# A planned order for chunk attention and a leaky-ReLU layer on one core: another load order at the start, half-wide first products, and copies planned apart from sums

## The chip, the core and the metric

The kernel runs on one core of a Trainium2 chip. The metric is the device time of one execution in microseconds (us); lower is better. The core has TensorE (PE in the profile) for matmuls, VectorE (DVE), ScalarE (ACT), GpSimd (POOL) and SyncE (SP), which each run their own list of instructions in order, and 16 DMA engines that are fed from queues. The loads are issued by POOL, the transposing copies and the stores by SP.

## The reference

```python
# q, k, v: (8, 8, 576, 64) float32; w_in: (512, 2048); w_out: (2048, 512)
def attn(q, k, v):                      # in chunks of 64 rows
    scores = (1 / sqrt(64)) * q_c @ k_c.T
    scores = scores - max(scores, axis=-1)
    attn = exp(scores); attn = attn / (sum(attn, axis=-1) + 1e-9)
    return attn @ v_c
x = attn_out.transpose(0, 2, 1, 3).reshape(4608, 512)
h = x @ w_in
g = maximum(0.01 * h, h)
out = (g @ w_out).astype(float32)
```

There are 72 chunks for each of 8 heads, and 4608 tokens go through the two layers. Inside the kernel the operands are float16, the sums float32.

## The kernel before

**Tiling.** A *group* u (0 to 35) is 128 tokens, two chunks of 64, all 8 heads. It goes through a chain of steps, each one instruction or a few: the loads (`arrive`, lines 776 to 782); the transposes of q and k, `pe_t`, on TensorE for u below `UD` = 10 (lines 400 to 408) and by a DMA on SP for the others (`t`, lines 421 to 432); the copies of the transposed q into a zero-padded tile QZ (`p`, lines 410 and 441); the scores `s` on TensorE (line 445, tile Sp); the largest value `m` and the difference `b` on VectorE; the exponential `x` on ScalarE; the sum and its reciprocal `z` on VectorE; the product `n` on VectorE or POOL (line 482, tile en); the transpose of the weights, `e` on TensorE and `d2` as its copy out, or `d` by a DMA on SP (lines 490 to 508, tile et); the product with v, `v` (line 510, tile xp); and `a` on ScalarE, which writes the 128 tokens into the ring xT (line 526).

**The two layers.** Tokens are handled in `BLOCKS`: four of 128 and eight of 512. Blocks 0 to 5 multiply plainly with w_in (`mm1`, line 176, 16 matmuls that are 128 columns wide), blocks 6 to 11 with a seven-product scheme (`f`, lines 307 to 325) that works on sums of quarter matrices: VF and WF are sums of the weights, XF sums of tokens (`x_form`, line 277), S sums of the hidden layer (`g_form`, line 336). Before the change a seven-product unit covers all 512 tokens of a block, so that one product is 4 matmuls of 256 columns. The second layer is plain for blocks 0 to 3 (`mm2`, line 205, in four parts of 4 matmuls, one for each quarter of w_out) and has the seven-product scheme for the others (`m2`, line 351, 8 matmuls of 256 columns).

**What sets the order.** Every step is an object with an engine, an assumed duration, the steps that it comes after, and a key. `run()` (line 626) plays the whole program with these durations and a model of the DMA queues, takes for each engine the ready step with the smallest key, and emits the instructions in that order. The result is a fixed list for each engine. On the chip each engine then follows its list, and waits wherever the data are not there. `TUNE` shifts keys and adds delays to single steps, `ON` moves single steps to another engine (it is empty before). Where the plan sees TensorE idle for over 0.4 us in its first 40 us, it puts in *fillers*: matmuls of the identity on itself (`idle`, line 531) whose results nothing uses.

**The start.** `front()` (line 795) gives the order of the first loads. A letter stands for a load: `Q` a quarter of w_in (two transfers of 256 KB in the tile), `P` a quarter of w_out (512 KB), `V` a 128-token tile of v that is then copied into place in eight or four pieces (`v_p`, line 128), `g` q and k of a group (128 KB each), `v` the v of the whole second batch, and `I` the identity, which all the transposes and fillers need. Group 0's q and k come by two other queues as float32.

Of the kernel before, what the change touches and what calls it, by code (L numbers as in the profile page):

```python
# [16 lines left out]
def kernel(  # L17
# [23 lines left out]
    UD = 10  # L41
# [11 lines left out]
    UNIT = {}  # L53
    POOL_N, POOL_X, POOL_S = 9, 20, 20
# [45 lines left out]
    def load_q(u):  # L100
        load_rows(q_tile(u), q, u)
        qk[u] = (q_tile(u), None)
# [127 lines left out]
    def minus(to, a, b):  # L230
        nc.vector.tensor_tensor(out=to, in0=a, in1=b, op=ALU.subtract)

    def plus(to, a, b):
        nc.vector.tensor_tensor(out=to, in0=a, in1=b, op=ALU.add)  # L234
# [5 lines left out]
    def out_form(i):  # L240
        if i == 0:
            minus(WF[:, 0], B12, B11)
        elif i == 1:
            minus(WF[:, 1], B22, WF[:, 0])
        elif i == 2:
            minus(WF[:, 2], B22, B12)
        else:
            minus(WF[:, 3], B21, WF[:, 1])
# [6 lines left out]
    def in_form(i):  # L255
        if i == 0:
            plus(VF[:, 0], W21, W22)
        elif i == 1:
            minus(VF[:, 1], VF[:, 0], W11)
        elif i == 2:  # L260
            minus(VF[:, 2], W11, W21)
        else:
            minus(VF[:, 3], W12, VF[:, 1])
# [362 lines left out]
    def run():  # L626
# [14 lines left out]
        of = {"pool": 0, "sp": 1}  # L641

# [43 lines left out]
        while True:  # L686
# [32 lines left out]
            now[s.eng] = s.issued  # L719
            can[s.eng].remove(s)  # L720
# [21 lines left out]
    FILL, FILL_TO, NEAR = 0.8, 40.0, 0.12  # L742
# [6 lines left out]
    TUNE = {('out', 0, 0): (-1, 0), ('pe_t', 8, 1): (2, 0), ('v', 5): (2, 0), ('s', 4): (-2, 0), ('m', 1): (0, 0.8), ('g', 1, 2, 0): (8, 1.2), ('mm2', 2, 0, 1): (0, 0.15), ('z', 5): (-4, 0), ('mm1', 2, 3, 0): (8, 0), ('pe_t', 5, 1): (2, 0), ('zv', 2, 0): (8, 0), ('a', 0): (-2, 0.5), ('b', 3): (0, 0.3), ('mm1', 0, 3, 0): (-8, 0), ('z', 2): (-8, 0), ('mm2', 3, 0, 0): (-2, 0), ('g', 2, 2, 0): (8, 0), ('v_p', 4, 1): (-1, 0), ('pe_t', 5, 0): (0, 0.8), ('v_p', 6, 1): (4, 0), ('v_p', 2, 0): (0, 1.2), ('mm2', 1, 0, 1): (0, 0.15)}  # L749
# [39 lines left out]
    ON = {}  # L789
# [5 lines left out]
    def front():  # L795
        for what in "Q0 I V0 g1 Q1 q2 k2 g3 V1 V2 Q2 P0 g4 V3 Q3 P1 P2 g6 g5 V4 v1 g7 P3".split():
# [3 lines left out]
            elif what[0] in "gqk":  # L800
                for i in ((0, 1) if what[0] == "g" else (0,) if what[0] == "q" else (1,)):
                    arrive(n[0], i)
            elif what[0] == "v":
                arrive_v(n[0], *(n[1:] or (0, NCH)))
            elif what[0] == "V":
                n = n[0]
                cs = [c for c in (2 * n, 2 * n + 1) if c < NCH]
                load(("v_t", n), 0.88, lambda n=n: load_v_rows(n), 510 * len(cs))
# [10 lines left out]
        for n, more in ((1, 500), (4, 700)):  # L819
# [9 lines left out]
        for i in range(4):  # L829
            for t in range(4):  # L830
                e, us = on(("zv", i, t), "dve", dve=0.3, act=0.6, pool=0.35)
                add(("zv", i, t), e, us, lambda i=i, t=t, e=e: zero(empty(i)[:, t], e, i % 2 * CH), key=8, at=(2.0, 2.5, 14.0, 14.0)[i])

    def group(u):
        at = 44.0 + BEGIN + (u - 5) * PACE if u >= 5 else 0.0
        k = u / 4
        dve = act = 10 + k - 1 * max(0, 5 - u)
# [23 lines left out]
        else:  # L861
            if not pairs:
                add(("t", u, 0), "sp", 1.28, lambda u=u: stage_t(u, 2), [get(("arrive", u, 0)), get(("p", u - 4, 0)), get(("p", u - 4, 1))], key=u).dmas = [(544, 1.0)]
                for s in range(2):
                    add(("p", u, s), "pool", 0.68, lambda u=u, s=s: stage_q2(u, s), [get(("t", u, 0)), get(("s", u - NQZ))], key=u / 100).slack = 0.0
# [21 lines left out]
        if by_pe:  # L887
# [12 lines left out]
        add(("v", u), "pe", 0.24, lambda u=u, h=h: stage_v(u, h.slot), need, key=-2, take=[h]).slack = 0.0 if by_pe else 1.0  # L900
# [116 lines left out]
    def second_fast(j, k0):  # L1017
# [4 lines left out]
        f2 = add(("sf", j, 2), *(("pool", 4.0) if j >= POOL_S else ("dve", 1.25)), lambda: g_form(j, 2), [f0] + g(0, 0), key=6.2 + k0)  # L1022
# [79 lines left out]
    BEGIN, PACE, SPARE, SPARE2, LEAN, LIMIT = -4, 4.8, 0, 0, 0.6, 3  # L1102
    front()
    for q_ in range(4):
        add(("wf", q_), "dve", 1.24, lambda q_=q_: out_form(q_), [get(("P", i)) for i in range(4)], key=9 + q_ / 10, at=44.0 + 8.0 + 3 * q_)
    for q_ in range(4):
        add(("vf", q_), "dve", 1.5, lambda q_=q_: in_form(q_), [get(("Q", 3, m)) for m in range(2)], key=9.5 + q_ / 10, at=44.0 + 8.0 + 15 + 3 * q_)
# [86 lines left out]
```

## Time and profile before

| | us |
|---|---|
| median of 3 runs | 280.42 (280.1 to 280.96) |
| the profiled execution | 279.68 |
| its span, first to last instruction | 277.5 |
| TensorE busy in the span | 266.2 (96%) |
| VectorE busy | 216.4 (78%) |
| ScalarE busy | 189.9 (68%) |
| POOL busy | 161.8 (58%) |

The page gives, for each engine, the time in which at least one of its instructions ran. Loads of weights into TensorE (PEld) run beside its matmuls (PE). A busy TensorE here includes the 135 fillers. In the rows of the timeline the columns are: start, duration, engine, line, operation, output and inputs, count of merged instructions, and in brackets the idle time before it and what ended that. A matmul's duration in a row is longer than its turn in the pipe, so the turn is read from one start to the next.

### The profile page before, as it was taken

What the parts mean: (1) busy time and instruction counts of PE and PEld (TensorE: products, weight loads), DVE (VectorE), ACT (ScalarE), POOL (GpSimd) and SP (SyncE); (2) the same over time, 40 slices, a digit from 0 to 9 for tenths busy, and PEclk for the clock granted to TensorE, in tenths of its full rate; (3) what the DMA queues carried; (4) which work ended last, traced back from release to release, by engine and by line L of the source; (5) the groups of instructions that cost most, each with busy time, mean ns of one, the idle gap of its engine ahead of it and who ended that gap; (6) DMA issues with size and microseconds to landing.
All of it is one profiled execution on the core that took longest, in us unless ns stands there. A gap on an engine that the chain in (4) does not pass through costs nothing.

```text
span 277.5 us, 7926 instructions
## 1 busy us (share of the span) xinstructions
PE 266.2 (96%) x3231; PEld 237.8 (86%) x3231; DVE 216.4 (78%) x382; ACT 189.9 (68%) x359; POOL 161.8 (58%) x194
## 2 busy tenths in 40 slices
PE   4899999999989999999999999999999999999995
PEld 3799957897988899989889988998999998888884
DVE  8678746999799959979997899799879963753372
ACT  3358854874763563799699749976977985795521
POOL 8765858729999999895976687775172210000000
PEclk9999999999999999999999999999999999999999
DMA  8999999999999999999999999999995210400133
GB/s 132 164 171 185 189 157 173 157 176 135 185 140 155 123 144 158 139 233 139 189 191 139 136 224 155 155 179 139 152 184 117 93 21 2 151 2 1 76 116 115
DMA packets 164180, 38.79 MB, mean 140 GB/s; under 512 B 155184, under 2 KB 159792, under 8 KB 164144
## 3 DMA queue, kind: packets, MB, share of 16 engines
q0 software_dynamic: 114384, 18.09, 102.7%
q1 hardware_dynamic: 48720, 19.93, 42.6%
q8 instruction: 25, 0.41, 0.6%
q10 hardware_dynamic: 1040, 0.26, 0.4%
q14 instruction: 11, 0.09, 0.1%
HBM read 36.70 MB, written 9.44 MB: 166 GB/s over the span
## 4 chain that ended last, share of the span: by engine, by line
PE 81%; DMA 6%; DVE 6%; POOL 3%; issue 1%; ACT 0%; DVEq 0%; POOLq 0%
PE oA L370 18%; PE hA L322 14%; PE hT L184 14%; PE oC L370 9%; PE hC L322 7%; PE oP L209 5%; PE hB L322 3%; PE oB L370 3%; DMA et<-en 3%; DMA k_in<-in_k_dram 3%; PE Sp L450 3%; PE xp L516 3%; DVE S L234 2%; DVE XF L282 1%; POOL w_inT L134 1%
## 5 line engine op out<-in xcount | busy, mean ns | idle before, releaser
L370 PEld LDWEIGHTS <-gT 128*128 128x128 f16 x640 | 61.5, 98 | 6.9
L184 PE MATMUL hT<-xT,w_inT 128*128 128x128 f16 x768 | 47.5, 219 | 0.3
L486 POOL TENSOR_TENSOR en<-ex,zi 128x512 f16<-128x512 f16 x27 | 29.7, 1102 | 29.6 <-DVE zi L480 16.3
L443 POOL COPY QZ<-QT 64x512 f16<-64x512 f16 x52 | 38.3, 737 | 12.5 <-DMA QT<-q_in 10.8
L184 PEld LDWEIGHTS <-w_inT 128*128 128x128 f16 x768 | 43.9, 98 | 1.4 <-PE idle L534 0.5
L322 PEld LDWEIGHTS <-VF 128*128 128x128 f16 x384 | 36.8, 98 | 4.7 <-issue 0.4
L234 DVE TENSOR_TENSOR tmp<-hC,tmp 128x512 f32<-128x512 f32 x48 | 31.9, 680 | 10.7 <-ACT tmp L198 5.3
L92 POOL DMA_DIRECT2D k_in<-in_k_dram x39 | 33.4, 859 | 6.9 <-DMA k_in<-in_k_dram 3.3
L92 POOL DMA_DIRECT2D q_in<-in_q_dram x39 | 33.5, 859 | 6.2 <-DMA q_in<-in_q_dram 1.4
L195 ACT ACTIVATE gT<-hT 128x512 f16<-128x512 f32 x48 | 28.1, 596 | 11.4 <-PE hT L184 10.9
L195 ACT ACTIVATE gT<-tmp 128x512 f16<-128x512 f32 x48 | 29.4, 640 | 7.0 <-DVE tmp L234 6.8
L470 ACT ACTIVATE ex<-sh 128x512 f16<-128x512 f32 x36 | 22.7, 630 | 14.2 <-DVE sh L464 10.3
L370 PE MATMUL oA<-WF,gT 128*128 128x256 f16 x256 | 31.7, 273 | 0.0
L198 ACT ACTIVATE tmp<-hA 128x512 f32<-128x512 f32 x48 | 28.2, 607 | 4.0 <-PE hA L322 4.0
L460 DVE TENSOR_REDUCE mx<-Sp 128x8 f32<-128x512 f32 x36 | 24.4, 678 | 7.7 <-PE Sp L450 7.3
L476 DVE TENSOR_REDUCE z<-ex 128x8 f32<-128x512 f16 x36 | 24.4, 677 | 7.7 <-ACT ex L470 7.6
L322 PEld LDWEIGHTS <-w_inT 128*128 128x128 f16 x288 | 27.6, 98 | 3.1
L529 ACT ACTIVATE xT<-xp 128x512 f16<-128x512 f32 x36 | 21.6, 599 | 11.5 <-PE xp L516 11.5
L322 PE MATMUL hA<-XF,VF 128*128 128x256 f16 x192 | 28.0, 273 | 0.0
L370 PEld LDWEIGHTS <-S 128*128 128x128 f16 x256 | 24.4, 98 | 3.6 <-DVE S L234 0.9
L198 ACT ACTIVATE tmp<-oA 128x512 f32<-128x512 f32 (+1 forms) x27 | 14.8, 547 | 17.9 <-PE oA L370 17.8
L464 DVE TENSOR_TENSOR sh<-Sp,mx 128x512 f32<-128x512 f32 x36 | 24.4, 679 | 0.4
(69 smaller groups left out, 491.6 us busy)
## 6 DMA issues: line engine op xcount, KB each, us to landing
out_dram<-osb SPq DMA_DIRECT2D x14, 512.0 KB, 5.7
VB<-in_v_dram POOLq DMA_DIRECT2D x14, 288.0 KB, 10.7
q_in<-in_q_dram POOLq DMA_DIRECT2D x31, 128.0 KB, 10.1
k_in<-in_k_dram POOLq DMA_DIRECT2D x31, 128.0 KB, 10.1
w_inT<-in_moe_w_in_dram POOLq DMA_DIRECT2D x8, 256.0 KB, 7.6
w_outT<-in_moe_w_out_dram POOLq DMA_DIRECT2D x4, 512.0 KB, 9.5
out_dram<-osb SPq DMA_DIRECT2D x6, 256.0 KB, 5.7
v_t<-in_v_dram POOLq DMA_DIRECT2D x4, 128.0 KB, 8.2
```

The costliest lines, as they stand in the source:

```text
L92: nc.gpsimd.dma_start(out=t[a - u * G:z - u * G], in_=src[b, :, r:r + z - a, :].rearrange("h p d -> p h d"))
L184: nc.tensor.matmul(out=hT[:, i, :], lhsT=w_inT[:, t, fc * 128:(fc + 1) * 128], rhs=xT[:, t, r0 % RING:r0 % RING + tb], start=(i == 0 and t ...
L195: nc.scalar.activation(out=to, in_=of, func=AFT.Prelu, bias=0.0, scale=1.0, alpha=0.01)
L198: nc.scalar.activation(out=to, in_=of, func=AFT.Copy, bias=0.0, scale=1.0)
L234: nc.vector.tensor_tensor(out=to, in0=a, in1=b, op=ALU.add)
L322: nc.tensor.matmul(out=PA[key][:, c, :], lhsT=w[:, t, fc * 128:(fc + 1) * 128], rhs=x[:, t, :], start=(m in (1, 5) and c == 0 and t == 0), ...
L370: nc.tensor.matmul(out=to, lhsT=lhs[:, fc, p * 128:(p + 1) * 128], rhs=rhs[:, fc, :], start=(fresh and fc == 0), stop=(fc == HB - 1), skip ...
L443: nc.gpsimd.tensor_copy(out=QZ[u % NQZ][part, :, :, s, :], in_=QT[u][part].rearrange("p i (e t) -> p i e t", e=2))
L460: nc.vector.tensor_reduce(out=MX[u], in_=SP[u], axis=AXL.X, op=ALU.max)
L464: nc.vector.tensor_tensor(out=SH[u], in0=SP.pop(u), in1=MX.pop(u).unsqueeze(2).to_broadcast((128, 8, CH)), op=ALU.subtract)
L476: nc.vector.tensor_reduce(out=z, in_=E[u], axis=AXL.X, op=ALU.add)
L486: eng.tensor_tensor(out=E[u], in0=ex, in1=ZI.pop(u).unsqueeze(2).to_broadcast((128, 8, CH)), op=ALU.mult)
```

## The change

1. **Start.** The load order becomes q1 k1 k2 Q0 I q2 q3 V0 V1 V2 k3 Q1 Q2 q5 V3 q4 P0 and so on: three groups' q and k ahead of most weights, the identity behind the first five transfers, Q3 near the end. Each part of `mm2` waits only for its own quarter of the hidden layer. The copies of v into place, the zeroing of tiles and the copies of q are spread over ScalarE, VectorE and POOL by `ON`.
2. **Fillers.** Their number is worked out from two rates: one for TensorE's slow first 4.3 us after the identity is there, one for afterwards. There are 86 in place of 135.
3. **Ports.** In the plan, POOL's copies and products (`p`, `n`, `v_p`, `zv`, `zq`) and VectorE's float16 sums (`wf`, `vf`, `sf`, `xf`) never run at the same time: a step with the flag `port` begins when the other engine's last such step has ended. No wait is added in the program for it.
4. **Width.** `UNIT` = 256 for blocks 6 to 11: a seven-product unit covers 256 tokens. A product is 8 matmuls of 128 columns; the sums XF are 48 instructions of 256 elements in place of 24 of 512.
5. **Engines.** `UE` = 8: the transposes `e` of groups 8 and 9 go from TensorE to a DMA on SP. VectorE makes 12 of the products `n` in place of 9, POOL 24 in place of 27. The slack that the plan keeps between a DMA transpose and the step `v` goes from 1.0 to 0.5 us.
6. **Pace and keys.** `BEGIN, PACE` = -6, 5.0 in place of -4, 4.8; `NEAR` 0.03 in place of 0.12; `TUNE` has entries over the whole program in place of its start alone.

```diff
-    UD = 10
+    UD, UE = 10, 8
...
-    UNIT = {}
-    POOL_N, POOL_X, POOL_S = 9, 20, 20
+    UNIT = {6: 256, 7: 256, 8: 256, 9: 256, 10: 256, 11: 256}
+    POOL_N, POOL_X, POOL_S = 10, 20, 20
...
-            return t
+            return max(t, port["dve" if s.eng == "pool" else "pool"]) if s.port else t
...
+            warm = done["I"].end + 4.3 if done["I"].end else INF
+            if s.eng == "pe" and t < warm:
+                s.us *= 1.8
...
-                    idle(int((t - a) * FILL / (0.0575 if a > done["I"].end + 4.5 else 0.12)), k[1])
+                    idle(int(max(0, min(t, warm) - a - 0.1) / 0.1065 + max(0, t - max(a, warm)) * FILL / 0.0575), k[1])
...
+            if s.port:
+                port[s.eng] = s.issued
...
+        s.port = s.eng == "dve" and name[0] in ("wf", "vf", "sf", "xf") or s.eng == "pool" and name[0] in ("p", "n", "v_p", "zv", "zq", "sf", "xf")
...
-        for what in "Q0 I V0 g1 Q1 q2 k2 g3 V1 V2 Q2 P0 g4 V3 Q3 P1 P2 g6 g5 V4 v1 g7 P3".split():
+        for what in "q1 k1 k2 Q0 I q2 q3 V0 V1 V2 k3 Q1 Q2 q5 V3 q4 P0 k5 P1 k4 q6 k7 V4 P2 k6 q7 Q3 v1 P3".split():
...
-        if by_pe:
+        if u < UE:
             h = Hold("bank")
             add(("e", u), "pe", 0.23, lambda u=u, h=h: stage_e(u, h.slot), [get(("n", u))], key=-2, take=[h])
...
-        add(("v", u), "pe", 0.24, lambda u=u, h=h: stage_v(u, h.slot), need, key=-2, take=[h]).slack = 0.0 if by_pe else 1.0
+        add(("v", u), "pe", 0.24, lambda u=u, h=h: stage_v(u, h.slot), need, key=-2, take=[h]).slack = 0.0 if by_pe else 0.5
...
-                        [s, get(("P", part))] + [x for key, v in G_OF.items() if key[0] == j for x in v], key=at, take=[hd] if part == 0 else [], spare=SPARE)
+                        [s, get(("P", part)), get(("g", j, part, 0))], key=at, take=[hd] if part == 0 else [], spare=SPARE)
...
-    BEGIN, PACE, SPARE, SPARE2, LEAN, LIMIT = -4, 4.8, 0, 0, 0.6, 3
+    BEGIN, PACE, SPARE, SPARE2, LEAN, LIMIT = -6, 5.0, 0, 0, 0.6, 3
```

More of the change, by code (lines that the diff above doesn't have):

```diff
@@ L101, in load_q @@
         load_rows(q_tile(u), q, u)
[L102 removed]
+        qk[u] = (q_tile(u), qk[u][1] if u in qk else None)
     def load_k(u):
@@ L641, in run @@
         of = {"pool": 0, "sp": 1}
+        port = {"dve": 0.0, "pool": 0.0}
         def release(s, which):
@@ L748 @@
     Step.slack = Step.hold = 0.0
-    TUNE = {('out', 0, 0): (-1, 0), ('pe_t', 8, 1): (2, 0), ('v', 5): (2, 0), ('s', 4): (-2, 0), ('m', 1): (0, 0.8), ('g', 1, 2, 0): (8, 1.2), ('mm2', 2, 0, 1): (0, 0.15), ('z', 5): (-4, 0), ('mm1', 2, 3, 0): (8, 0), ('pe_t', 5, 1): (2, 0), ('zv', 2, 0): (8, 0), ('a', 0): (-2, 0.5), ('b', 3): (0, 0.3), ('mm1', 0, 3, 0): (-8, 0), ('z', 2): (-8, 0), ('mm2', 3, 0, 0): (-2, 0), ('g', 2, 2, 0): (8, 0), ('v_p', 4, 1): (-1, 0), ('pe_t', 5, 0): (0, 0.8), ('v_p', 6, 1): (4, 0), ('v_p', 2, 0): (0, 1.2), ('mm2', 1, 0, 1): (0, 0.15)}
+    Step.port = False
@@ L807, in front @@
                 cs = [c for c in (2 * n, 2 * n + 1) if c < NCH]
-                load(("v_t", n), 0.88, lambda n=n: load_v_rows(n), 510 * len(cs))
+                load(("v_t", n), 0.88, lambda n=n: load_v_rows(n), 560 * len(cs))
                 for c in cs:
@@ L818, in front @@
                 load(("P", n[0]), 1.0, lambda a=n[0]: load_w_out(a), 2930)
-        for n, more in ((1, 500), (4, 700)):
+        for n, more in ((1, 500), (4, 700)) if arrivals[0].name[0] != "Q" else ((0, 1300), (1, -200)):
             arrivals[n].dmas = [(p + more / len(arrivals[n].dmas), y) for p, y in arrivals[n].dmas]
@@ L831, in front @@
                 e, us = on(("zv", i, t), "dve", dve=0.3, act=0.6, pool=0.35)
-                add(("zv", i, t), e, us, lambda i=i, t=t, e=e: zero(empty(i)[:, t], e, i % 2 * CH), key=8, at=(2.0, 2.5, 14.0, 14.0)[i])
+                add(("zv", i, t), e, us, lambda i=i, t=t, e=e: zero(empty(i)[:, t], e, i % 2 * CH), key=8, at=(2.0, 2.5, 20.0, 22.0)[i])
     def group(u):
@@ L836, in group @@
         k = u / 4
-        dve = act = 10 + k - 1 * max(0, 5 - u)
+        dve = act = 10 + k - 0.5 * max(0, 5 - u)
         by_pe = u < UD
@@ L864, in group @@
                 for s in range(2):
-                    add(("p", u, s), "pool", 0.68, lambda u=u, s=s: stage_q2(u, s), [get(("t", u, 0)), get(("s", u - NQZ))], key=u / 100).slack = 0.0
+                    add(("p", u, s), "pool", 0.62, lambda u=u, s=s: stage_q2(u, s), [get(("t", u, 0)), get(("s", u - NQZ))], key=u / 100).slack = 0.0
             elif u % 2 == 0:
@@ L1021, in second_fast @@
         f1 = add(("sf", j, 1), "dve", 1.25, lambda: g_form(j, 1), [f0] + g(0, 0) + [get(("m2", j - 1, 6, p)) for p in range(2)], key=6 + k0)
-        f2 = add(("sf", j, 2), *(("pool", 4.0) if j >= POOL_S else ("dve", 1.25)), lambda: g_form(j, 2), [f0] + g(0, 0), key=6.2 + k0)
+        f2 = add(("sf", j, 2), *(("pool", 4.0) if j >= POOL_S else ("dve", 1.25)), lambda: g_form(j, 2), [f0] + g(0, 0), key=6.6 + k0)
         wf = [get(("wf", q)) for q in range(4)]
```

39 lines of the change are left out of this document (21 added, 18 removed).

## The prediction

> **What bounds the kernel now.** I read the page first, for the engines and the 40 slices.
>
> ```profile
> span 277.5 us, 7926 instructions
> PE 266.2 (96%) x3231; PEld 237.8 (86%) x3231; DVE 216.4 (78%) x382; ACT 189.9 (68%) x359; POOL 161.8 (58%) x194
> ...
> PE   4899999999989999999999999999999999999995
> ...
> DVE  8678746999799959979997899799879963753372
> ...
> POOL 8765858729999999895976687775172210000000
> ```
>
> TensorE is busy from the second slice to the last. VectorE and POOL are full only in stretches (POOL from 62 to 118 us). So the end is set by TensorE: by the work that it must do, and by the time in which it does none. The waits of TensorE (who, for what: us in total, times, longest), without those of the first 11 us, show the second kind after the start:
>
> ```profile
> PE Sp L450 <- POOL QZ L443: 0.9, 1, 0.9
> ...
> PE oC L370 <- DVE S L234: 0.6, 2, 0.4
> PE xp L516 <- DMA et<-en: 0.6, 1, 0.6
> PE hC L322 <- DVE osb L234: 0.2, 1, 0.2
> ```
>
> That is 2.3 us in all. The start is another matter: its busy time is mostly fillers. The timeline of TensorE:
>
> ```profile
> 3.29 1.25 PE L534 MATMUL idle<-ident 128*128 128x128 f16 x10 [3.29 <-POOL ident masks.py:199]
> ...
> 5.29 0.60 PE L403 MATMUL qp<-ident,q_in 128*128 128x128 f16 x4 [0.75 <-DVE q_in L537]
> ...
> 7.72 2.11 PE L534 MATMUL idle<-ident 128*128 128x128 f16 x18
> 10.91 0.61 PE L403 MATMUL qp<-ident,q_in 128*128 128x128 f16 x4 [1.07 <-DMA q_in<-in_q_dram]
> ...
> 15.34 1.28 PE L534 MATMUL idle<-ident 128*128 128x128 f16 x20
> 16.77 1.05 PE L184 MATMUL hT<-xT,w_inT 128*128 128x128 f16 x16
> ...
> 27.75 0.40 PE L450 MATMUL Sp<-KT,QZ 128*128 128x64 f16 x8
> 27.98 0.39 PE L403 MATMUL qp<-ident,q_in 128*128 128x128 f16 x4
> ...
> 29.29 1.95 PE L184 MATMUL hT<-xT,w_inT 128*128 128x128 f16 x32
> ```
>
> The last filler ends at 29.29 us; behind it nothing but work follows. The groups of TensorE in the window 0 to 29.27 us say what was done by then:
>
> ```profile
> L534 PE MATMUL idle<-ident 128*128 128x128 f16 x135 | 13.0, 263 | 3.3 <-POOL ident masks.py:199 3.3
> L184 PE MATMUL hT<-xT,w_inT 128*128 128x128 f16 x96 | 6.0, 220 | 0.2
> L408 PE MATMUL kp<-ident,k_in 128*128 128x128 f16 x20 | 2.4, 256 | 0.1
> L403 PE MATMUL qp<-ident,q_in 128*128 128x128 f16 x20 | 2.4, 255 | 1.8 <-DMA q_in<-in_q_dram 1.1 <-DVE q_in L537 0.7
> L450 PE MATMUL Sp<-KT,QZ 128*128 128x64 f16 x32 | 1.8, 206 | 0.2
> L494 PE MATMUL tpe<-ident,en 128*128 128x128 f16 x12 | 1.4, 250 | 0.1
> L516 PE MATMUL xp<-et,VB 128*128 128x64 f16 x24 | 1.2, 193 | 0.1
> ```
>
> The turns in the pipe come from the chain of work that ended last:
>
> ```profile
> 31.47 3.57 PE hT L184 x64
> 35.27 1.73 PE oP L209 x8
> ...
> 267.46 5.24 PE oA L370 x48
> ```
>
> 128 columns take 3.57/64 = 55.8 ns, 256 columns 5.24/48 = 109.2 ns. The eight Sp matmuls from 27.75 to 27.98 take 0.23 us. At these turns the window holds 148 matmuls of 128 columns (8.3 us) and 7 steps of eight small ones (1.6 us): 9.9 us of work in 29.3 us. **The start loses 19.4 us**; the waits lose 2.3. The change is weighed on three terms: this loss, the work, and the waits.
>
> **The start.** What the first matmuls of a layer wait for is loads, so I need their pace. POOL holds eight transfers in the air and waits with the next for the oldest; its timeline therefore dates the landings:
>
> ```profile
> 9.62 0.87 POOL L92 DMA_DIRECT2D q_in<-in_q_dram  x1 [0.59 <-DMA w_inT<-in_moe_w_in_dram]
> ...
> 16.05 0.75 POOL L140 DMA_DIRECT2D w_outT<-in_moe_w_out_dram  x1 [0.30 <-DMA q_in<-in_q_dram]
> ...
> 26.18 1.49 POOL L140 DMA_DIRECT2D w_outT<-in_moe_w_out_dram  x2 [1.91 <-DMA w_outT<-in_moe_w_out_dram]
> ...
> 33.99 1.15 POOL L110 DMA_DIRECT2D VB<-in_v_dram  x1 [0.74 <-DMA w_outT<-in_moe_w_out_dram]
> 36.49 0.88 POOL L92 DMA_DIRECT2D q_in<-in_q_dram  x1 [1.36 <-DMA w_outT<-in_moe_w_out_dram]
> ```
>
> By these rows, eight transfers back each time, Q0 was there at 9.6, P0 at 26.1, P1 at 34.0, P2 at 36.5. So a P takes 2.5 us. Between Q0 and P0 nine 128 KB tiles, four halves of a Q and P0 landed in 16.5 us; between P0 and P1 three tiles, two halves and P1 in 7.9. Two equations: a tile takes 1.1 us, a half of Q 1.0 us.
>
> The new order by these paces, counted back from Q0's two halves (the queue's zero is at 7.6): k2 10.9, Q0 12.9, q2 and q3 15.1, V0 16.2, V1 17.3, V2 18.4, k3 19.5, Q1 21.5, Q2 23.5, P0 29.3, P1 32.9, P2 39.2, Q3 43.4. This is the late end: the zero holds the time in which group 0's q and k load beside them, and small tiles that go first may be through up to 1.5 us sooner. I take the middle, 0.8 earlier.
>
> The identity moves behind three issues of 0.87 us: ready at 5.9 in place of 3.3. That costs little, as group 0's q reached TensorE only at 5.3.
>
> Which step starts TensorE's packed stretch? Its new list has 86 fillers, all ahead of `e` of group 1; then v0, the transpose of k3, v1 and the first mm1. ScalarE's list has a(0) behind two copies that read V2, and POOL's list has three copies that read V1, behind the issue of V3, which stands eight transfers back and so waits for V1.
>
> ```profile
> 10.05 1.69 ACT L117 ACTIVATE VB<-v_t 64x256 f16<-64x256 f16 x4
> ...
> 15.54 0.60 ACT L529 ACTIVATE xT<-xp 128x512 f16<-128x512 f32 x1 [1.16 <-PE xp L516]
> ```
>
> By ScalarE: V2 at 17.6, two copies of 0.42, a of 0.60, 0.2 for the handing on: 19.2. By POOL: V1 at 16.5, issue 0.87, three copies, each between the 0.42 of ScalarE and the 0.61 of POOL's QZ copy of twice the size (below): 18.6 to 19.2, then v1 with 0.23. By k3: 18.7 and its transpose. So mm1 starts at 19.4 (18.4 with the tiles 1.5 sooner, 20.3 with k3 at 19.5). By then 10 transposes, 3 scores and 2 products with v are done, 3.4 us. Loss 16.0.
>
> After that TensorE has no fillers and each landing comes close ahead of its user. Walking its list with the turns above: v2 waits some 0.2 for d2 on ScalarE, mm2 of P0 and P1 and the transpose of q6 come within 0.3 of their landings; Q3 (42.6) is used first behind 27.2 us of work, at 43.8; v of group 4 is used behind 30.4 us of work, at 47.0, and v1 lands by 46.5. I add 0.6 (0.2 to 1.2). **16.6 in place of 19.4: -2.8** (-4.2 to -1.3). Here mm2 by quarters is the cover: until Q3 comes, the parts of P0 to P2 for four groups, 12 steps of 1.73/2 = 0.87 us, 10.4 in all, fill the place that Q3's 3.6 us had.
>
> **The work.** 672 matmuls of 256 columns become 1344 of 128: 2 x 55.8 - 109.2 = 2.4 ns each time, +1.6 us, none of it covered, since TensorE is the bound. Two groups' `e` go: 8 x 55.8 = -0.45. **+1.15.** Their d go onto SP's queue ahead of later transposes:
>
> ```profile
> L443 POOL COPY QZ<-QT x52: 599/612/1599, 62.4 to 208.0; 64x512 f16<-64x512 f16 x52
> ...
> L505 SPq DMA_TRANSPOSE et<-en x26: 1188/1296/3108, 79.4 to 224.3; - x26
> ...
> DMA to landing us min/median/max: 2.4/7.7/9.5
> ...
> L234 DVE TENSOR_TENSOR S<-gT x8: 1211/1266/2160, 76.2 to 263.7; 128x2048 f16<-128x2048 f16 x8
> ...
> L282 DVE TENSOR_TENSOR XF<-xT x12: 374/414/1966, 112.2 to 234.8; 128x512 f16<-128x512 f16 x12
> ```
>
> That is 1.3 us of SP each (min/median/max in the second row, ns) and a landing after 7.7; queued behind are the transposes of groups 12 to 14, and v8 and v9 wait for them. Cover: in the new list v8 stands behind 53.9 us of work in place of 50.4, v9 behind 61.5 in place of 53.7. The sums XF: 414 ns for 512 elements and 1.21 us for 2048 give 0.28 us for 256, so 48 x 0.28 - 24 x 0.414 = +3.5 us on VectorE over 130 us, where its slices show 3 to 7 tenths at several places. Gain: a unit of 256 tokens starts when two groups are there, not four.
>
> **The waits.** In these rows a QZ copy takes 0.61 and up to 1.60, a sum S 1.21 and up to 2.16, an XF 0.41 and up to 1.97. Three of the four waits above, 1.7 of 2.3 us, have such a copy or sum, or a sum behind one, as their cause. The Trainium skill, page "SBUF — State Buffer", says that GpSimd and a VectorE operation with two SBUF inputs share one port pair, and that whichever starts first holds it for its whole instruction while the other waits; the stretched rows agree with that. By that rule a plan that truly keeps them apart removes all 1.7. But only the planned times keep them apart, nothing in the program does, and I expect part of it: 1.2 left of 2.3, **-1.1** (between 0.3 and 4 left). Against it, v after a DMA transpose has 0.5 us less slack. In its favour, TensorE's list asks for the groups later: s16 behind 81.0 us of work (75.9 before), v28 behind 189.5 (172.6), so although TensorE is 2.8 us further on, most groups are due no sooner.
>
> **Sum.** -2.8 + 1.15 - 1.1 = -2.75. The profiled execution took 279.68 (2.2 around its span); 276.9 by the sum. It lies 0.7 under the median of the runs, 280.42, from which I count: **277.7**.
>
> **Rivals.**
> - *The ports are kept apart in the plan only.* If the lists drift by the length of a copy, copies meet sums as before. The waits stay at 2.3: 278.8. For it: no wait enforces it. Chance 0.15.
> - *The clock falls back.* The fillers ran at 2.11/18 = 117 ns at 7.72 and 64 ns at 15.34; from the gap of 1.07 us it took 3.9 us or more to come up. In the new start some 1.5 us of idling lies among v0, k3 and v1; if that counts, the next 3.9 us run at half rate and cost 2.0: 279.7. The page "TensorE: Matmul & The Clock Gate" of the Trainium skill, Part 1, asks for a whole idle window of about 3.4 us before the clock drops; by that rule this case is not reached, and no row here shows a warm array going cold. Chance 0.10.
> - *The start is only rearranged.* The first mm1 moves from 16.8 to 20.3, the packed stretch has holes where P and Q3 come, and the loss stays 19.4: 280.4. Against it: the old start has fillers between its hT rows up to 29.29, the new list none behind its first mm1. Chance 0.10.
> - *Slower: the DMA transposes land late.* They take 7.7 us in the median and up to 9.5; the plan now allows 0.5 us in place of 1.0, and TensorE stands still with all its list behind xp. With six of the 28 such groups late by 0.8 us the waits are 6 us: 282.5. It decides from 3.9 us of waits on (no gain), and makes it slower from 4.8. For it: one such wait of 0.6 with the larger slack. Against: v stands later in the list. Chance 0.17.
>
> **The numbers.** My forecast has 0.48. About 0.3%, 0.8 us, is what a measurement here can tell from no change. Faster: 0.48, 0.13 of the first rival, 0.01 of the others: 0.62. Within 0.3%: half of the second and third, some of the first: 0.13. Slower: the last rival and the rest: 0.25. The range: the early start with 0.3 of waits left, -4.2 + 1.15 - 2.0 = -5.05, gives 275.4; the late one with 3.6 of waits, -1.3 + 1.15 + 1.3, gives 281.6, which leaves out the worst of the last rival.
>
> **What would show it.** Right: the last filler before 18 us, the first hT at 19 to 20, no wait over 0.5 us from there to 45; turns of 55 to 56 ns on L322; QZ copies and S sums nearer to 612 and 1211. Wrong: fillers or waits that bring the start's loss back to 19; waits of xp for et of several us; hT at over 100 ns after 19 us; or L322 at over 58 ns.

## The result, and the profile after

The changed kernel is slower: 284.28 us (median of 4, 283.07 to 284.65), the kernel before 280.28 beside it (280.10 to 280.96); ratio 1.0131, 95% interval 1.0095 to 1.0167. The forecast was 277.7, range 275.4 to 281.6. Single executions of one kernel spread by some 6 us at most here: the medians below hold all of them, while the ratios leave out those over 1.5% above their kernel's fastest, which would lower the median of e10 by 2.2 us and the others by at most 0.7.

The page after (profiled execution 283.07):

```profile
span 281.3 us, 9167 instructions
PE 263.4 (94%) x3846; PEld 242.2 (86%) x3846; DVE 217.5 (77%) x391; ACT 198.3 (70%) x366; POOL 160.0 (57%) x200
...
PE   1999999999999999999978889999999999999994
...
DVE  5894287987998599789967889999898884844731
...
POOL 8999884967986938586287777964344022000000
...
DMA  9999999999999999999999999999999302400133
```

TensorE, without a hole behind the start before, now has one at 140 to 170 us. The last row, the busy share of the DMA engines, is at 9 up to 218 us; so it was before, to 208 us, and the prediction did not use it:

```profile
DMA  8999999999999999999999999999995210400133
```

The row stops at 9 and counts the time of every packet, of which several are in the air at once. So it can't say how much room is left; the experiments have to.

TensorE's waits (who, for what: us in total, times, longest):

```profile
PE Sp L450 <- POOL QZ L443: 2.8, 2, 2.5
PE xp L516 <- DMA et<-en: 2.3, 5, 0.8
PE oC L370 <- DVE S L234: 1.2, 1, 1.2
PE kp L408 <- DMA k_in<-in_k_dram: 1.0, 2, 0.5
```

The start in its timeline (start, duration, instruction, count, idle time before):

```profile
6.02 0.58 PE L408 MATMUL kp<-ident,k_in 128*128 128x128 f16 x4 [6.02 <-POOL ident masks.py:199]
...
15.92 1.23 PE L534 MATMUL idle<-ident 128*128 128x128 f16 x19
...
18.27 0.40 PE L408 MATMUL kp<-ident,k_in 128*128 128x128 f16 x4 [0.46 <-DMA k_in<-in_k_dram]
...
18.74 1.96 PE L184 MATMUL hT<-xT,w_inT 128*128 128x128 f16 x32
```

The last filler ends at 17.2, the first hT is at 18.74: the start came as forecast. The time was lost later. The windows view says where (window, length, busy us and count of PE, PEld, DVE, ACT and POOL, granted clock, DMA share, GB/s; the DMA share passes 1 where packets overlap), first before, then after:

```profile
130.00:180.00 50.00, 49.35 (x551) 44.31 (x549) 44.51 (x75) 40.96 (x78) 36.62 (x44) 1.00 1.68 169
```

```profile
130.00:180.00 50.00, 45.06 (x683) 42.05 (x681) 42.57 (x76) 37.11 (x69) 35.91 (x44) 1.00 1.75 156
```

4.3 us of TensorE's busy time are gone in these 50 us alone. The chain of waits before the largest stall of the changed kernel (start, length, what):

```profile
119.83 0.88 POOL q_in L92
120.71 19.54 DMA k_in<-in_k_dram
...
140.53 0.88 POOL k_in L92
...
142.43 0.87 POOL q_in L92
...
144.44 0.46 POOL en L486
...
146.39 1.05 POOL en L486
147.45 0.56 POOL QZ L443
...
148.05 0.62 POOL QZ L443
...
148.72 0.41 PE Sp L450 x8
```

A load of keys takes 19.5 us to land. POOL may have eight loads in the air (in this trace no issue starts with more than seven others under way), so it waits with the next ones, and the products n of groups 20 and 21 and the QZ copies of group 23, behind them in its list, come late. The score s of group 23 waits 2.5 us for them. In the views of DMA issues the loads of one shape (count, KB, median us to landing) went from the first line, before, to the second, after:

```profile
k_in<-in_k_dram POOLq DMA_DIRECT2D x31, 128.0 KB, 10.1
```

```profile
k_in<-in_k_dram POOLq DMA_DIRECT2D x31, 128.0 KB, 13.0
```

The two traces part between 80 and 100 us. Counted in the DMA records of that stretch: 13,337 load packets before and 9,079 after, 4,595 and 5,326 packets of transposes, none and 256 of stores. The first half-wide product starts at 105.2 us, so this parting is not the width's doing. From then on each load of groups 17 to 28 lands 3.5 to 21 us later than before.

### The profile page after: what moved, and what is told of

The parts are those of the page before. It is cut to its first block, busy times and chain, and to the rows that moved or that the text cites. A ratio compares the mean times of both kernels' runs of the same rounds, so it can differ in the third digit from the quotient of the medians.

```text
span 281.3 us, 9167 instructions
## 1 busy us (share of the span) xinstructions
PE 263.4 (94%) x3846; PEld 242.2 (86%) x3846; DVE 217.5 (77%) x391; ACT 198.3 (70%) x366; POOL 160.0 (57%) x200
## 4 chain that ended last, share of the span: by engine, by line
PE 55%; DMA 22%; POOL 9%; ACT 5%; DVE 4%; issue 2%; SPq 1%; POOLq 0%; DVEq 0%; ACTq 0%
PE oA L370 11%; DMA k_in<-in_k_dram 10%; PE hA L322 10%; DMA et<-en 9%; PE hT L184 7%; PE oC L370 7%; PE oP L209 5%; PE hC L322 5%; PE oB L370 3%; DMA QT<-q_in 3%; ACT gT L195 2%; PE hB L322 2%; POOL q_in L92 2%; PE xp L516 2%; POOL en L486 2%
## 5 line engine op out<-in xcount | busy, mean ns | idle before, releaser
L370 PEld LDWEIGHTS <-gT 128*128 128x128 f16 x640 | 60.2, 98 | 6.2
L322 PEld LDWEIGHTS <-VF 128*128 128x128 f16 x768 | 46.3, 98 | 0.5
L184 PEld LDWEIGHTS <-w_inT 128*128 128x128 f16 x768 | 43.9, 98 | 1.0
L443 POOL COPY QZ<-QT 64x512 f16<-64x512 f16 x52 | 34.1, 656 | 15.9 <-DMA QT<-q_in 12.5
L486 POOL TENSOR_TENSOR en<-ex,zi 128x512 f16<-128x512 f16 x24 | 27.1, 1132 | 24.4 <-ACT tmp L198 12.4
L195 ACT ACTIVATE gT<-hT 128x512 f16<-128x512 f32 x48 | 27.9, 598 | 15.4 <-PE hT L184 15.2
L322 PEld LDWEIGHTS <-w_inT 128*128 128x128 f16 x576 | 35.3, 98 | 0.4
L322 PE MATMUL hA<-XF,VF 128*128 128x128 f16 x384 | 28.0, 219 | 0.0
## 6 DMA issues: line engine op xcount, KB each, us to landing
q_in<-in_q_dram POOLq DMA_DIRECT2D x31, 128.0 KB, 11.5
```

Of the source, the lines that this page charges most:

```text
L184: nc.tensor.matmul(out=hT[:, i, :], lhsT=w_inT[:, t, fc * 128:(fc + 1) * 128], rhs=xT[:, t, r0 % RING:r0 % RING + tb], start=(i == 0 and t ...
L195: nc.scalar.activation(out=to, in_=of, func=AFT.Prelu, bias=0.0, scale=1.0, alpha=0.01)
L322: nc.tensor.matmul(out=PA[key][:, c, :], lhsT=w[:, t, fc * 128:(fc + 1) * 128], rhs=x[:, t, :], start=(m in (1, 5) and c == 0 and t == 0), ...
L370: nc.tensor.matmul(out=to, lhsT=lhs[:, fc, p * 128:(p + 1) * 128], rhs=rhs[:, fc, :], start=(fresh and fc == 0), stop=(fc == HB - 1), skip ...
L443: nc.gpsimd.tensor_copy(out=QZ[u % NQZ][part, :, :, s, :], in_=QT[u][part].rearrange("p i (e t) -> p i e t", e=2))
L486: eng.tensor_tensor(out=E[u], in0=ex, in1=ZI.pop(u).unsqueeze(2).to_broadcast((128, 8, CH)), op=ALU.mult)
```

## The experiments

The terms below come from one profiled execution of each kernel. Start loss: the first 30 us less the work done in them, as in the prediction. Waits: from 30 us on, every TensorE step's time until the next step begins, less its turn. Tail: from the last matmul to the end of the span. That execution lies up to 2 us from its kernel's median (the changed kernel's 1.2 below it, e2's 1.9 above), so the terms are no sharper than that. The waits of e1, e6, e9, e10 and e13 hold 1.6 to 1.7 us of matmuls at half clock (last section).

| kernel | median us (n) | before beside it | start loss | work | waits | tail |
|---|---|---|---|---|---|---|
| before | 280.28 (4) | | 19.4 | 251.1 | 4.0 | 3.1 |
| changed | 284.28 (4) | 280.28 | 16.0 | 252.3 | 9.2 | 3.8 |
| e1 loads behind | 284.20 (10) | 280.13 | 15.6 | 252.3 | 11.5 | 3.7 |
| e2 less v | 276.43 (4) | 280.13 | 18.8 | 252.3 | 1.9 | 3.5 |
| e3 other order | 286.84 (4) | 280.13 | 15.4 | 252.3 | 12.9 | 3.5 |
| e4 width alone | 283.77 (4) | 280.13 | 19.1 | 252.8 | 5.1 | 3.1 |
| e5 before split | 282.82 (6) | 280.47 | 19.1 | 252.8 | 5.4 | 3.1 |
| e6 after, pairs | 279.01 (10) | 280.47 | 15.4 | 250.6 | 8.9 | 3.6 |
| e8 before, less v | 279.06 (10) | 280.47 | 18.3 | 251.1 | 2.9 | 3.1 |
| e9 both off | 277.48 (4) | 280.69 | 15.7 | 250.6 | 6.9 | 3.5 |
| e10 wide, e on TensorE | 283.00 (10) | 280.69 | 19.1 | 251.1 | 8.4 | 3.1 |
| e11 refit | 280.31 (10) | 280.69 | 19.2 | 252.5 | 2.5 | 4.5 |
| e12 refit, no port rule | 280.19 (10) | 280.69 | 18.6 | 252.3 | 4.3 | 4.1 |
| e13 start kept, no port rule | 280.09 (12) | 280.32 | 17.6 | 252.3 | 6.3 | 3.8 |
| e14 start kept, port rule | 277.01 (6) | 280.32 | 16.0 | 252.5 | 2.5 | 3.6 |

(e7, 282.25 in 11 executions: its profiled one took 286.75, too far from the median to stand for it, and is left out.)

**e1: is it POOL's list?** After planning, six load issues are emitted behind the copies that they held up:

```diff
...
+        behind([('arrive', 26, 1), ('arrive', 27, 0), ('arrive', 27, 1), ('arrive', 28, 0), ('arrive', 28, 1), ('arrive', 29, 0)], ("p", 23, 1))
...
```

> The changed kernel with its own order, except that six load issues on POOL (the keys of group 26, q and k of 27 and 28, q of 29) stand behind n20, n21 and the two QZ copies of group 23 instead of ahead of them. Nothing else moves. Theory (POOL's list is blocked at load issues that need the landing of the eighth load before them, and the copies and n steps queued behind them come late): n20 follows s20 by under 18 us instead of 24.7, the 2.64 us wait before s23 at 145 us falls under 0.6, the waits of v21, v22 and m2(7,5,0) shrink with it, and the time falls by 2 to 5 us from 284.3, to 279.3 to 282.3. The DMA queue never runs empty, so the loads themselves land no later than 1 us after where they land in the changed kernel. Rival A (the DMA queue is late whatever POOL does, so that the same wait comes back at t26, t27 and their groups): s23's wait goes, waits from 155 us on grow by as much, time within 1 us of 284.3. Rival B (the loss sits in the 256-wide units or their instruction fetches, or in the ports): time unchanged, 283.5 to 285.

Time unchanged (ratio to before 1.0093, 1.0050 to 1.0135). n of group 20 came at 139.9 and not 145.5, the last QZ copy of group 23 at 143.7 and not 148.7, and s of group 23 waited for nothing. But the transposes that follow landed no sooner, and TensorE waited there (timeline of e1):

```profile
152.20 0.41 PE L450 MATMUL Sp<-KT,QZ 128*128 128x64 f16 x8 [1.41 <-POOL QZ L443]
...
157.19 0.41 PE L516 MATMUL xp<-et,VB 128*128 128x64 f16 x8 [2.37 <-DMA et<-en]
```

My theory of the blocked list falls as the cause; rival A holds. The place of these six load issues decided only which step waits. (Rival B named the same time; e5 and e6 take up the width and the fetches.) What is short would then be DMA time, which e2 tests.

**e2: take load off the DMA engines.**

```diff
-            x = load(("v_in", b, c0, m), 1.14, lambda m=m: load_v(b, m, c0, c1), 256 * (c1 - c0), after, **kw)
+            x = load(("v_in", b, c0, m), 1.14, lambda m=m: b in (4, 5) or load_v(b, m, c0, c1), 256 * (c1 - c0), after, **kw)
```

> The changed kernel with its own order, leaving out the four loads of v for batches 4 and 5 (they are not issued; those groups then use the values of older batches). That takes 4 x 2304 packets, some 8 us of the load queue at the 1200 packets per us that it shows alone and up to 11 us at the shared rate, out of the stretch from 105 to 150 us. Theory (loads land late because the queue has more to move than the order allows for, and POOL blocks on them): the loads of groups 22 to 28 land 5 to 11 us earlier, POOL's waits ahead of load issues fall from 22 to under 14 us, s23 waits under 0.6 us, the time falls by 3 to 6 us to 278.3 to 281.3. Rival B (width, fetches or ports): no change beyond 1 us. Rival C (any order misses by some us, wherever it is disturbed): the waits move to other steps and the time stays within 1.5 us.

7.9 us less, more than expected, with the order untouched: the waits go from 9.2 to 1.9, and the loads of groups 17 to 29 land some 9 us earlier on average. The waits list of e2 has nothing large behind the start; its 2.1 us fall at 25 us, inside the start, whose loss was 18.8 in this execution:

```profile
PE tpe L494 <- DVE en L486: 2.1, 1, 2.1
PE kp L408 <- DMA k_in<-in_k_dram: 0.9, 1, 0.9
PE xp L516 <- DMA et<-en: 0.5, 1, 0.5
```

**e8: the same in the kernel before** (the same edit).

> The kernel before with its own order, leaving out the four loads of v for batches 4 and 5, as in the run that took 8 us off the changed kernel. Theory (the kernel before runs at the same limit, with a little more room): its waits after 30 us fall from 4.0 to between 1.0 and 2.5, time 280.1 - 1.0 to 3.0, 277.1 to 279.1, so that the two kernels without those loads lie within 2.5 us of each other and the changed one, at 276.4, is ahead. Rival (only the changed kernel's order is short of loads): before's time within 0.7 us of 280.1.

-1.4 us: at the upper end of the theory's band (279.06), but the 95% interval of the ratio, 0.9934 to 1.0007, just includes no change, and the waits of 2.9 are above the 1.0 to 2.5 expected. At most some 2 us of the kernel before hang on these loads, against 7.9 of the changed one: it has more room. Without them the changed kernel is the faster one by 2.6 us, about what it gained at the start less its work (3.4 - 1.2).

**e3, e4: another order, and the width alone.** e3 keeps `TUNE` and `ON` for the start only; e4 is before with one line changed:

```diff
-    UNIT = {}
+    UNIT = {6: 256, 7: 256, 8: 256, 9: 256, 10: 256, 11: 256}
```

> The changed kernel's rules (port rule, 256-wide units, transposes of e from group 8 on by DMA, slacks, the same start), but the fitted keys and the choice of engine kept only for the start (groups under 8, blocks 0 to 3); the rest falls back to the usual keys, so that the order after about 60 us is another one. Its own plan ends at 270.38 against 270.20 for the changed kernel. If the loss after 30 us belongs to the rules (width, port rule, e by DMA), it comes back: 283 to 286. If it belongs to the one order (which load issue stands ahead of which copy), the time may come out anywhere between 279 and 288, with the waits at other steps than s23, v21, v22 and m2(7,5,0).

> The kernel before with one edit: blocks 6 to 11 in units of 256 tokens (128 columns in a product) as in the changed kernel; its start, its ports and its other settings stay. Its own plan ends at 272.68 against 270.92. If the width costs only its columns (1344 matmuls at 55.8 ns for 672 at 109.2, +1.6 us, less what the finer grain saves), the time is 280.3 plus 1.0 to 3.0, 281.3 to 283.3, the work term of the ledger rises by 1.2 to 1.7 us and the rest is waits of the new order. If five more fetches of instructions and the shorter instructions make TensorE or the load queue late by themselves, the waits after 30 us rise by 4 us or more as in the changed kernel (from 4.0 to 8 or more), and the time is 285 or more.

e3: 286.84, waits of 12.9 us, at s14, s23, v26 and v30. That is above the 283 to 286 of the first case and inside the 279 to 288 of the second, so e3 doesn't tell the rules from the order. e4: +3.6 us, between the two cases that I had named; work +1.7, waits +1.2 in the profiled execution. Both change the order as well, so neither is clean. The next two hold it.

**e5, e6: the width with the order held.** e5 issues each 256-column matmul of before's in-products as two of 128; e6 does the reverse in the changed kernel:

```diff
-            for t in range(HT2):
...
+            for y in (slice(0, 128), slice(128, 256)):
+                for t in range(HT2):
+                    nc.tensor.matmul(
+                        out=PA[key][:, c, y], lhsT=w[:, t, fc * 128:(fc + 1) * 128], rhs=x[:, t, y],
...
```

```diff
-            for t in range(HT2):
+            for t in range(HT2) if c % 2 == 0 else ():
...
-                    out=PA[key][:, c, :], lhsT=w[:, t, fc * 128:(fc + 1) * 128], rhs=x[:, t, :],
+                    out=PA[key][:, c:c + 2, :], lhsT=w[:, t, fc * 128:(fc + 1) * 128],
+                    rhs=x[:, t, :].unsqueeze(1).to_broadcast((128, 2, n)),
```

> The kernel before with its own order on every engine, and one edit: each matmul of 256 columns of the fast in-products is issued as two of 128 (same result, 672 matmuls more). Work: 1344 x 55.8 ns less 672 x 109.2 ns is +1.6 us. Instruction fetches: one 16 KB fetch for every 128 matmuls, so 25 become 30, and during each the load and transpose queues together fall for about 1 us from 820-1200 to some 250 packets per us. Theory (both kernels are short of DMA time from 80 to 200 us, so that each fetch makes loads later and TensorE waits): waits after 30 us rise from 4.0 by 1 to 4 us and the time to 280.1 + 2.6 to 5.6, 282.7 to 285.7. Rival (the order alone made the waits, the fetches are beside the path): +1.6 us of work and waits within 0.6 of before's, 281.2 to 282.3.

> The changed kernel with its own order, and the reverse edit: the two matmuls of 128 columns that use neighbouring blocks of weights are replaced by one of 256 columns, which reads the same 128 columns of x twice and leaves the second block of weights out. Half the in-product matmuls are gone (672 for 1344), work 1.6 us less, fetches 25 for 30. Theory: the waits after 30 us fall from 9.2 by 1 to 3 us beside the 1.6 us, time 284.3 - 2.6 to 4.6, 279.7 to 281.7. Rival (order alone): 284.3 - 1.6 and the waits as they are, 282.2 to 283.2.

e5: +2.35 us, between the theory (+2.6 or more) and the rival (+2.2 at most); the interval of its ratio, 1.0042 to 1.0145, is +1.2 to +4.1 us. e6: -5.3 us, beyond the theory's upper end (ratio to before 0.9963, 0.9930 to 0.9997). 1.6 us of each is work. The rest is 0.8 us in the kernel before, which the noise doesn't tell from none, and 3.7 in the changed one, which is clear of it.

That this rest is DMA time is likely and not shown. In e6's profiled execution (280.26, 1.2 above its median) the waits were 8.9 and not 6.2 to 8.2, and the loads of groups 17 to 29 land 1.2 us earlier than in the changed kernel, those of 30 to 35 3.0; in e5's the loads of 17 to 29 land 0.5 us earlier than before's, not later. No run changed the fetches of instructions alone. What speaks for them stands in the queue rows of the two pages, before and after:

```profile
q8 instruction: 25, 0.41, 0.6%
```

```profile
q8 instruction: 30, 0.49, 0.7%
```

These are fetches of 16 KB of TensorE's instructions, one for every 128 matmuls. Counted in the DMA records around the 16 fetches between 60 and 200 us of the changed kernel, in bins of 0.4 us (each named by its start), the packets of loads, transposes and stores together end

```
us from the fetch's end   -1.8  -1.4  -1.0  -0.6  -0.2  +0.2  +0.6  +1.0  +1.4
packets per us             889   842   800   657   264   119   362   761   852
```

so around each fetch some 800 packets are missing, most of one group's q or k load (1,024). Five more fetches are 4,000 packets, 4.5 to 5 us of the queues at the 800 to 890 per us beside them (an estimate).

**e7, e9: the transposes of e.** e7 leaves out the two DMA transposes that `UE` = 8 added; e9 is e6 and e7 at once.

```diff
+        if u in (8, 9):
+            E.pop(u)
+            ET[u] = None
+            return
...
```

> The changed kernel with its own order, leaving out the two DMA transposes of e of groups 8 and 9 (which the kernel before makes on TensorE); those two groups' products with v read zeros. 1088 packets go out of the stretch from 64 to 92 us, 2.6 us of the time in which loads run at about 410 packets per us and not at 1200, so that some 2100 load packets come through earlier. Theory: the loads of groups 17 to 22 land 1.5 to 4 us earlier, the waits after 30 us fall from 9.2 by 1 to 2.5 us, time 281.8 to 283.3. Rival (two transposes are lost in a queue that has room; the order alone makes the waits): time within 0.6 us of 284.3.

> The changed kernel with its own order and both edits of the two runs before at once: 672 in-product matmuls of 256 columns for 1344 of 128 (leaving every second block of weights out), and no DMA transposes of e for groups 8 and 9 (their products with v read zeros). Alone they took off 5.3 and 2.0 us. What is left of the change is its start and its order. Theory (three loads on one limit, the start's gain of 3.4 us being real and covered up): waits after 30 us under 5, the time 276.3 to 278.3, that is 2.1 to 4.1 us under the kernel before. Rival (the order itself keeps some 4 us of waits that no relief takes): 279 to 281.

e7: -2.0 us, as expected (ratio to before 1.0040, 1.0008 to 1.0072). Whether the loads landed earlier, as it expected too, its trace can't say: that execution took 286.75, and in it they land later. e9: 277.48, ratio to before 0.9883 (0.9844 to 0.9921); the two single effects sum to 277.0. So the change is the start's gain, with some 7 us of cost from two edits that I had priced at 1.15. The waits of e9's profiled execution were 6.9 and not under 5: 2.0 us at s23 stayed, and 1.7 were matmuls at half clock behind it (the last section has another such case).

**e10 to e12: plan with the right DMA rates.** The planner's model has no fetches and lets loads run at 549 packets per us beside a store; the records show some 150 to 170. It gets the rates that the traces show, and the keys are fitted anew to that:

```diff
+            w = 0.25 if any(a <= self.now + 1e-9 < b for a, b in self.stalls) else 1.0
-                return (549.0, 399.0 / h[1][2]) if h[1][2] > 1 else (419.0, 399.0)
+                return (170.0 * w, 150.0 * w) if h[1][2] > 1 else (415.0 * w, 415.0 * w)
...
+                if (fetched[0] + c - 20) // 128 > (fetched[0] - 20) // 128:
+                    dma.stalls.append((t, t + 1.0))
```

> The changed kernel without its two loads on the DMA engines: in-products in units of 512 tokens (256 columns) and e of groups 8 and 9 transposed on TensorE, as before; its start and its port rule stay. The order is planned anew, with a DMA model set to this case's traces (415 load and 415 transpose packets per us when both queues have work, 1200 loads alone, 170 and 150 beside a store, a quarter of that for 1 us at each fetch, one fetch per 128 matmuls), and its keys fitted to that. Full result. Theory: start loss 16 to 17 us, waits after 30 us 2 to 4, work 251, the time 276 to 278.5, faster than both. Rival (any new order misses by 4 us somewhere): 279.5 to 283.

> The changed kernel with its 256-token units kept and only e of group 8 taken back to TensorE (e of group 9 on by DMA); copies of QZ and n from group 11 on POOL; order planned anew with the DMA model set to the traces as in the run beside it, keys fitted to that. Full result. If the planner's DMA model is what failed (no fetches in it, stores too cheap), an order made with it holds on the chip although the loads on the DMA engines are nearly the same: waits after 30 us 1 to 3.5, the time 275.5 to 278.5. If the 256-token units cost 4 us in any order: 280 to 283.

> The changed kernel with 256-token units and e by DMA from group 8 on, as it is, but without the port rule (POOL's copies may run beside VectorE's fp16 sums), and with v planned 1.5 us behind its transpose instead of 0.5; order planned anew with the DMA model set to the traces, keys fitted to that. Full result. Theory (DMA time is the limit, the ports are not): waits after 30 us 1 to 3.5, the time 275.5 to 278.5; more QZ copies and sums overlap than in the changed kernel and are longer, without moving the end. Rival (the ports matter once the DMA waits are gone): 1 to 2 us slower than the run beside it that keeps the rule. Rival (256-token units with e by DMA from group 8 cost their 5 to 7 us in any order): 281 to 284.

e10 missed: its ratio to before is 1.0017 (0.9978 to 1.0055), with waits of 8.4 us, 3.3 of them at one transpose of e, and the start lost. I have no cause for that one order. e11 and e12 brought the waits down to 2.5 and 4.3 at nearly the full load, but the fit had moved the start as well and lost its 3 us, so both only equal the kernel before, and miss the times I expected.

**e13, e14: the start kept.** As e12 and e11 with the start's list held, instruction for instruction, up to 31 us; e14 has `UE` = 9, `POOL_N` = 8, `BEGIN` = -4 and the port rule, e13 `UE` = 8 and no port rule; each has keys of its own.

> The changed kernel's start, kept instruction for instruction on every engine up to 31 us, and its loads on the DMA engines kept too (256-token units, e by DMA from group 8 on); what comes later is planned anew with the DMA model set to the traces (a fetch for every 128 matmuls, 415 and 415 packets per us shared, 1200 for loads alone, 170 and 150 beside a store), with keys fitted to that, and without the port rule. Full result. The two refits before held their waits at 2.5 and 4.3 us, but had lost the start (19.2 and 18.6 us, against 16.0). Theory (the order made with a wrong DMA model is what failed; start and waits add up): start loss 15.7 to 16.5, waits after 30 us 2 to 4.5, time 276.5 to 279.0, below both kernels. Rival (the early start itself moves the later stages into the shortage, so that its gain is lost in waits whatever the order): waits 6 to 8, time 280 to 282.

> As the run beside it (the changed kernel's start kept, the rest planned anew with the DMA model set to the traces), but with the port rule kept, and e by DMA from group 9 on. Full result. Theory: start loss 15.7 to 16.5, waits 2 to 4.5, time 276.5 to 279.0. If the ports matter once the DMA waits are small, it is 0.5 to 1.5 us faster than the run beside it; if not, within 0.8 us of it.

**e14 beats both kernels: 277.01, ratio to before 0.9872 (0.9823 to 0.9921).** Start loss 16.0, waits 2.5. Its row of the windows view and of the key loads:

```profile
130.00:180.00 50.00, 49.35 (x750) 46.96 (x748) 46.31 (x85) 41.08 (x79) 39.36 (x48) 1.00 1.91 148
```

```profile
k_in<-in_k_dram POOLq DMA_DIRECT2D x31, 128.0 KB, 9.4
```

The half-wide products, the early start and one of the two added transposes are in it; so nearly the same load on the DMA engines fits, in an order whose loads of groups 17 to 29 land 10.9 us earlier than the changed kernel's. Which of its settings did that is not shown. e13, without the port rule, stays at 280.09, with waits of 6.3 us: it misses what I expected and gives the rival's numbers, which e14, with the same start, does not. Its largest wait, 2.2 us of s12 for QZ, is a port case; chain of e13:

```profile
79.87 1.55 POOL QZ L443
...
81.47 1.70 POOL QZ L443
...
83.22 0.61 PE Sp L450 x8
```

Two copies of 0.61 us took 1.55 and 1.70, beside a sum of 1.47 us (from 79.48) and one of 1.21 (from 81.47) on VectorE. That the port rule is worth the 3 us between e13 and e14 isn't shown, since their orders differ too; that two such meetings made its chain some 2 us longer is.

## Why the prediction was wrong

- **Start, -2.8: right.** 19.4 became 16.0, -3.4. The first hT was forecast at 18.4 to 20.3 and came at 18.74; the last filler ended at 17.2 (before 18). No wait reached 0.5 us from there to 45 us. k3 landed at 18.2, Q1 at 20.0, P0 at 27.6, Q3 at 40.8: 0.5 to 1.8 us ahead of the middle that I took (18.7, 20.7, 28.5, 42.6); P0 and Q3 came 0.2 and 1.1 us before the early end.
- **Work, +1.15: right as far as it went.** +1.2 by the table. The turns of L322 are 56 ns, as forecast: 16 of them in 0.89 us of the chain.

```profile
241.22 0.89 PE hA L322 x16
```

- **Waits, -1.1: wrong, and this is the step that failed.** They rose by 5.2 us (4.0 to 9.2 in the table, which also counts the gaps too small for the list of 2.3). I costed the two `d` as 1.3 us of SP and a landing, and the width as columns on TensorE and sums on VectorE, and put what either does to the other loads at nothing. The price was 2.0 us for the two `d` (e7), and 3.7 us beside the work for the width (e6); both off, the time falls by 6.8 us to 277.48 (e9), of which 1.7 are work and some 5 the price that I had at nothing. That the changed kernel is short of DMA time is shown by e2; that the width's 3.7 us come by the fetches is argued. The cover that I named, that TensorE's list asks for the groups later, looked at demand alone: s23 stands behind 6.5 us more work, but its loads land 9.4 and 10.6 us later.
- **Ports: the rule did part of its work.** QZ copies that overlap a sum fell from 18 to 14 of 52, their longest from 1.60 to 1.51 us, their mean from 737 to 656 ns. But one port wait is among the largest of the changed kernel, the 1.2 us for S: that sum took 2.06 us beside two products n on POOL, and TensorE waited for it.

```profile
164.64 2.09 POOL L486 TENSOR_TENSOR en<-ex,zi 128x512 f16<-128x512 f16 x2
165.75 2.06 DVE L234 TENSOR_TENSOR S<-gT 128x2048 f16<-128x2048 f16 x1
167.87 1.05 PE L370 MATMUL oC<-WF,S 128*128 128x256 f16 x8 [1.16 <-DVE S L234]
```

- **The slower rival** had the right sign and the wrong place. It named transposes of e that land late, because the plan's slack was cut. Those waits were 2.3 us and not 6; the largest was Sp for QZ, by loads.
- **The clock rival** didn't occur at the start, but later (below).
- **Not in the sum at all:** the tail, +0.7, and the fetches.

## What to carry to other kernels

When a kernel's DMA engines show 9 in nearly every slice, ask what a transfer keeps from the others and not only what its own latency is. The row doesn't answer that: leave out some loads, and see what the whole time does (7.9 us in one kernel here, 1.4 in the other). Count the instructions that feed TensorE as well: halving a matmul's columns doubles them, and cost 3.7 us beyond the work here. An order can also be planned with the DMA rates of the trace while what already works (the start) is held; of five orders planned with those rates, two of which held the start, one beat the kernel before, and the others only equalled it.

## What the runs showed of the hardware that I had not expected

**An instruction fetch stalls the other DMA queues.** The rates stand above: from some 800 packets per us to 119 at the lowest, for about 1.4 us. The Trainium skill, page "Runtime: NRT & Kernel Launch", section "Instruction fetch mechanics", says that a sequencer fetches the next 16 KiB through a DMA queue of its own and that the cost is mostly hidden. No wait in TensorE's lists above is put down to a fetch; for the loads beside it, it isn't hidden.

**Loads and transposes take turns.** With both queues at work, each ends about 410 packets per us (430 of loads and 390 of transposes in the median of the 0.4 us bins between 60 and 200 us of the kernel before), while loads alone reach 1,200: by these rates one transpose of e, 544 packets, keeps about 1,000 load packets back (an estimate).

**The clock falls after waits of 2 us.** In e13, TensorE stood still from 81.1 to 83.2 us (windows view, columns as above, the clock third from the right):

```profile
81.00:82.00 1.00, 0.05 (x1) 0.00 (x0) 1.00 (x2) 0.36 (x1) 0.94 (x2) 1.00 5.15 151
82.00:83.00 1.00, 0.00 (x0) 0.00 (x0) 0.68 (x1) 1.00 (x3) 1.00 (x1) 1.00 1.15 75
83.00:84.00 1.00, 0.78 (x10) 0.71 (x11) 0.14 (x1) 0.25 (x1) 1.00 (x2) 0.59 2.48 158
84.00:85.00 1.00, 1.00 (x7) 0.71 (x5) 1.00 (x2) 0.00 (x0) 0.96 (x3) 0.50 2.40 155
85.00:86.00 1.00, 1.00 (x10) 0.88 (x9) 0.86 (x4) 0.00 (x0) 0.94 (x2) 0.50 1.77 158
86.00:87.00 1.00, 1.00 (x16) 1.00 (x15) 1.00 (x3) 0.00 (x0) 1.00 (x2) 0.70 1.83 156
```

The clock is at half rate for 3.4 us, which adds 1.7 us to a wait of 2.2. The same followed in e1, e6, e7, e9 and e10 after waits of 1.5 to 3.3 us, but not after the 2.5 us of the changed kernel's profiled execution. The Trainium skill, page "TensorE: Matmul & The Clock Gate", Part 1, asks for a whole idle window of some 3.4 us. Here 2.2 us were enough in e13 and 2.0 at s23 in e9, while 2.5 us at s23 were not in the changed kernel.

The clock records of the traces say a little more. After the start, the clock changes only at whole multiples of 3.41 us from its first rise (20 of them, 68.27 us, to the drop in e13; 37, 126.29 us, in e10), and each drop lasts 3.41 us. Counted on that grid with the turns of the matmuls, TensorE worked in 1 to 39% of the stretch ahead of each of the six drops, and in 47% or more of all other stretches at full clock in the sixteen traces, but for one: the changed kernel's with the 2.5 us wait, at 38%. So where a wait falls matters; the exact condition stays open. Two of the changed kernel's four executions have a mean granted clock of 0.994, which is what one such drop in 283 us gives; they took 284.55 and 284.65 us, the other two, at 1.000, 283.07 and 284.01.
